# Attention and spectral mixing on one core: the order of kept products, the source of the causal masks, and when two tables are loaded

## The chip, the cores and the metric

The kernel runs on one core of a Trainium2 chip. The metric is device time in microseconds (us) from one execution of the whole program; the kernel before takes 436.24 us, the median of 3 runs (435.94 to 436.30).

A core has a matrix engine (PE, with its weight loads shown as PEld), a vector engine (DVE), a scalar engine (ACT), GpSimd (Pool) and a queue engine (SP). Each takes its instructions in the order in which the program wrote them and waits, where it must, for the others. Loads and stores are issued by SP or Pool and carried out by 16 DMA engines.

## What is computed

Attention over 8 batches x 8 heads, 576 positions, head size 64, with a causal mask and a bias from a running sum of s; its output, put together as x of 8 x 576 x 512, goes through a spectral mixing layer with 64 modes:

```python
scores = scale * np.matmul(q, k.transpose(0, 1, 3, 2))
cum = np.cumsum(np.maximum(s, 0.0), axis=-1)
bias = -(cum[:, :, :, None] - cum[:, :, None, :])
scores = np.where(causal, -1000000000.0, scores + np.minimum(bias, 0.0))
attn = softmax(scores)
x = (attn @ v).transpose(0, 2, 1, 3).reshape(B, S, H * D)

X = np.fft.rfft(x, axis=1)[:, :n_modes]
Yr = einsum('bmd,mde->bme', Xr, w_r) - einsum('bmd,mde->bme', Xi, w_i)
Yi = einsum('bmd,mde->bme', Xr, w_i) + einsum('bmd,mde->bme', Xi, w_r)
y = np.fft.irfft(Y, n=S, axis=1)
u = x + y
out = u + np.maximum(u @ w_ch, 0.0)
```

The weights w_r and w_i, 64 x 512 x 512 numbers each, are by far the largest inputs.

## The kernel before

**Loads.** Pool issues all large loads, through `load` (L311, the DMA at L315): q, k and v of the coming steps and, between them, the weights w_r and w_i, which are turned into 16-bit numbers on the way. The order is written out by hand; which weights may be asked for is limited by `fits` (L326), which looks at the places in SBUF that earlier weights still hold. SP issues the small ones at the start, in this order: s, the identity, `negm` (L348), then, after Pool's first loads in the text, the forward table `Ff_sb` (L352) and the inverse table `G_sb` (L353). Behind these on SP come rows of the running sum for the first steps (L444), a copy of it to DRAM (L720), and later one row load per step (L441).

**Attention.** 32 steps n, one for a batch and a pair of heads, four groups of 8 steps. A step transposes q and k on PE (L454, copied out at L458), and `scores` (L480) forms the scores in PSUM. The causal mask is added by PE: an identity times a slice of `negm` opens each accumulation (L493, L496, and L467 for the tail positions), then the products of q and k follow (L504), then ACT's exponential (L513). `negm` is a 128 x 581 table of 0 and -1e9 in three parts (`NMB` = 258, `NMA` = 259, `NL` = 64 columns), read through shifted windows. It is computed on the host, lies in DRAM as a constant, and is loaded once. `fft` (L567) multiplies x by the table `Ff_sb` one step later.

**Mode products.** The products with w_r and w_i for groups 0 to 2 run inside the attention steps. Those of the last group follow after it, in 8 chunks c of 8 modes: `modes(g, c)` (L619) makes 16 products (L628) in four quarters, two with w_r and two with w_i, then asks Pool for the next weights that now have a place, then adds the earlier groups' sum and writes `y_sb` (L651). Given `meanwhile`, a function is called ahead of a numbered quarter, and its work is put there on PE. `y_transposed` (L839) turns a chunk round for the product with w_ch; `gather_round` (L857) moves several chunks' rows, as they are and times w_ch, into `yv` through PSUM and copies by ACT and DVE (L876).

**Kept products.** Of the 18 pairs of output tiles, 16 have x times w_ch made ahead. Six are made in the last attention steps; ten later: `x_transposed` (L803, copied by DVE at L813), then `keep` (L827), which multiplies (L822) and lets ACT put the result away (L684). `work()` (L882) does the transpose of the next pair and the product of the pair before it. `late[-1]`, the tenth, is done by itself. Pairs 0 and 1 are not kept: their products stay in PSUM.

The order of the last group's work is given by a loop over c, with `TAKE` as the number of `work()` calls in each round:

```python
for x in range(TAKE[c] - 1):
    work()
...
yt = y_transposed(yb, c)
if TAKE[c]:
    work()
```

With `TAKE = (2, 2, 3, 0, 0, 0)` eight calls stand before chunk 3's products, two more behind chunk 4's. Chunks 0 and 1 stand together at the start, chunks 2 and 3 after more calls each.

**The end.** A tiny DMA, `mark` (L1036), waits on SP for the last weights; behind it the rows of chunk 6 are spread into `yv` (L662). The last chunk's quarters have `first_z(1)` and `first_u` between them (L1047). Its result is transposed (L1054), multiplied by w_ch (L1061) and added to the first outputs (L919), and then a list of steps written out by hand makes all outputs: x and the inverse transform into PSUM (L938, L908), ACT's relu or copies (L961, L959, L1073), sums on Pool (L964) and DVE (L976, L978), and the stores (L985).

Of the kernel before, what the change touches and what calls it, by code (L numbers as in the profile page):

```python
# [14 lines left out]
ALU = mybir.AluOpType  # L15
# [4 lines left out]
def kernel(  # L20
# [11 lines left out]
    nc = tc.nc  # L32
    B, H, S, D = q.shape
    NM = moe_w_r.shape[0]
    DM = H * D
    P = 128
# [26 lines left out]


    ident_np = np.eye(P, dtype=np.float32)
    row = np.arange(P)[:, None]
    key_b = RV * (row % (P // 2)) + row // (P // 2)
    key_a = np.where(row < P // 2, -RV, RV * row - W)
    NMB, NMA = W + RV - 2, W + RV - 1
    negm_np = np.concatenate(  # L70
        [
            np.where(key_b > np.arange(NMB)[None, :] - (RV - 2), -1.0e9, 0.0),
            np.where(key_a > np.arange(NMA)[None, :] - (RV - 1), -1.0e9, 0.0),
        ],
        axis=1,
    )
    nat = np.arange(NL)
    negm4_np = np.concatenate([np.where(nat[:, None] > nat[None, :], -1.0e9, 0.0)] * 2, axis=0)
    t_idx = np.arange(S, dtype=np.float64)
    m_idx = np.arange(NM, dtype=np.float64)  # L80
    ang = 2.0 * np.pi * np.outer(t_idx, m_idx) / S
# [7 lines left out]
    G_np = np.ascontiguousarray(G_np.reshape(P, SP)[:, :S].astype(np.float16))  # L89

    d_ident16h = nc.inline_tensor(ident_np.astype(np.float16), name="c_ident16h").ap()
    d_negm = nc.inline_tensor(
        np.concatenate([negm_np, negm4_np], axis=1).astype(ml_dtypes.bfloat16), name="c_negm"
    ).ap()
    Ff_np = np.ascontiguousarray(Ff_np.reshape(NT, P, 2 * NM).transpose(1, 0, 2).reshape(P, -1))
    d_Ff = nc.inline_tensor(Ff_np, name="c_Ffwd").ap()
    d_G = nc.inline_tensor(G_np, name="c_Ginv").ap()
# [247 lines left out]

    nc.sync.dma_start(out=s_sb, in_=s.rearrange("b h t -> (b h) t"))
    nc.sync.dma_start(out=ident16h, in_=d_ident16h)
    nc.sync.dma_start(out=negm[:, : NMB + NMA + NL], in_=d_negm)  # L348
    first = loads_qk(0)
    load(first[:2])  # L350
    load(loads_w(2 * W0), loads_v(0) + loads_tails(0) + first[2:] + loads_v(1))
    nc.sync.dma_start(out=Ff_sb.rearrange("p T c -> p (T c)"), in_=d_Ff)  # L352
    nc.sync.dma_start(out=G_sb[:, :S], in_=d_G)  # L353

    def keys_of(t, x):

# [78 lines left out]
    def cum_rows(n):  # L435
        if n >= N:
            return
        g, b = divmod(n, B)
        p0 = b * H + 2 * g
        if n >= 2:  # L440
            nc.sync.dma_start(out=qt[n % NQ][D : D + 1, :, :], in_=ncum_dram[p0 : p0 + 2, :S].unsqueeze(0))  # L441
            return
        for h in range(2):
            nc.sync.dma_start(out=qt[n % NQ][D : D + 1, h, :], in_=ncum_sb[p0 + h : p0 + h + 1, :])  # L444

    def transposes(n, half):
        if n >= N:
            return
        src = loaded[n][:, n % 2, :].rearrange("p (r d) -> p r d", d=D)[:, half * RH : half * RH + RH]
        ps = trpool.tile([P, RH, 2 * RP], BF16, name="tr_ps", tag="tr")  # L450
        for r in range(RH):
            for i in range(2):
                rows = slice(HP * i, HP * i + HP)
                nc.tensor.transpose(ps[rows, r, :], src[rows, r, :], ident16[rows, rows])  # L454
        for i, dst in enumerate((qt, kt)):
            copy = (nc.vector.tensor_copy, nc.scalar.copy)[half * i]
            to = dst[n % NQ][:D].rearrange("d h (p r) -> d h p r", r=R)
            copy(  # L458
                out=to[:, :, :, half * RH : half * RH + RH],
                in_=ps[HP * i : HP * i + HP].rearrange("d r (h p) -> d h p r", h=2),  # L460
            )
# [254 lines left out]
    with tc.tile_pool(name="sc_psum", bufs=2, space=PSUM) as scpool, \  # L716
            tc.tile_pool(name="tr_psum", bufs=1, space=PSUM) as trpool, \
            tc.tile_pool(name="av_psum", bufs=1, space=PSUM) as avpool:
        cum_rows(0)
        nc.sync.dma_start(out=ncum_dram[:, :S], in_=ncum_sb)  # L720
        transposes(0, 0)
        transposes(0, 1)
        load(loads_qk(2) + loads_v(2))
        pad_p()
        for n in range(N):
            tails_due = loads_tails(n // B + 1)[n % B - 3 : n % B - 2] if 2 < n % B < 5 else []
            load((loads_qk(n + LA) if n % 2 else []) + (loads_vs(n) if n else loads_v(LA)) + tails_due, loads_w(on_chip[n]))
            if n == N - B:
                nc.gpsimd.dma_start(out=wch_sb, in_=moe_w_ch.rearrange("(dt p) e -> p dt e", p=P))
            cum_rows(n + 1)  # L730
            scores(n, 0)
            if n and n % B == 0:
                av(n - 1, 1)
                v_place(n)
                scores(n, 1)
                transposes(n + 1, 0)
                fft(n - 1)
                av(n, 0)
                fft_pick(n - 1)
                transposes(n + 1, 1)  # L740
                mode_products(n)
                continue
            av(n - 1, 1)
            mode_products(n)
            transposes(n + 1, 0)
            v_place(n)
            scores(n, 1)
            i = first_pairs[n - N + len(first_pairs)] if n >= N - len(first_pairs) else None
            if i is not None:
                first_transposed(i, 0)  # L750
            transposes(n + 1, 1)
            fft(n - 1)
            av(n, 0)
            fft_pick(n - 1)
            if i is not None:
                first_product(i, 0)
                if n == N - 1:
                    av(n, 1)
                first_transposed(i, 1)
                if n == N - 1:  # L760
                    fft(n)
                first_product(i, 1)
        fft_pick(N - 1)
# [39 lines left out]
    def x_transposed(i):  # L803
        xts[i] = xt_sb[len(xts) % 3]
        for x, (b, T) in enumerate(pairs[i]):
            ps = upool.tile([P, DT, P], FP32, name="xt_ps", tag="u")
            for rows, bb, ident in parts(b, T):
                for dt in range(DT):
                    nc.tensor.matmul(
                        ps[:, dt, rows], x_all[: rows.stop - rows.start, dt, bb, T, :],  # L810
                        ident, start=True, stop=True, skip_group_check=True,
                    )
            nc.vector.tensor_copy(out=xts[i][:, x], in_=ps)  # L813
# [25 lines left out]
    def y_transposed(yb, c=NCK):  # L839
        ps = auxpool.tile([P, DT, P], FP16, name="yt_ps", tag="aux")  # L840
        for dt in range(DT):
            nc.tensor.transpose(ps[:, dt, :], yb[:, bass.ts(dt, P)], ident16h)
        yt = yt_first[:, :, c % NY, :] if c < NCK - 2 else spool.tile([P, DT, P], FP16, name="yt_sb", tag="yt")
        nc.scalar.copy(out=yt, in_=ps)
        return yt
# [36 lines left out]
    def work():  # L882

        if not order_z and not ahead:
            return
        if order_z:
            i = order_z.pop(0)
            x_transposed(i)
            ahead.append(i)
        if len(ahead) == 2 or not order_z:  # L890
            i = ahead.pop(0)
            keep(i)

    late = [i for i in kept if i not in first_pairs]
    order_z = late[:-1]
    TAKE = (2, 2, 3, 0, 0, 0)
    us, rs = {}, {}
    last = len(pairs) - 1
    x_pool = ()
# [87 lines left out]
    def z_of(i):  # L987
        return [zs[i, x] for x in range(2)]

    AHEAD = 3  # L990
    ybs = {}
    work()
    for c in range(NCK - 2):
        for x in (c, c + 1):
            if x not in ybs and (x == c or x < AHEAD):
                ybs[x] = modes(NG - 1, x)
        yb = ybs[c]
        for x in range(TAKE[c] - 1):
            work()
        if c == NCK - 3:  # L1000
            x_transposed(late[-1])
            x_transposed(0)
        yt = y_transposed(yb, c)
        if TAKE[c]:
            work()
        if c >= NY:
            if c == NCK - 3:
                x_times_wch(0, False)
                x_transposed(1)
                for which, pool in ((1, auxpool), (0, upool)):  # L1010
                    for x in range(2):
                        gather_round(NY, NCK - 2, 4 * x, which, pool)("sv"[x])
        elif c == NY - 1:
            modes(NG - 1, NY, ris=(0,))
            for x, pool in enumerate((auxpool, upool, auxpool, auxpool)):
                if x == 2:
                    ybs[NY] = modes(NG - 1, NY, ris=(1,))
                for which in (1, 0):
                    gather_round(0, NY, 2 * x, which, pool)()
                if x >= 2:  # L1020
                    work()
    assert not order_z and not ahead
    c = NCK - 2
    yb6 = modes(NG - 1, c, {2: lambda: keep(late[-1])})
    x_times_wch(1, False, (0,))
    yt = y_transposed(yb6)
    x_times_wch(1, False, (1,))
    vb6 = y_times_wch(c, yt)


    def first_u():
# [107 lines left out]
```

## Time and profile before

| | us |
|---|---|
| median of 3 runs | 436.24 |
| the profiled execution | 437.91 |
| its span, first to last instruction | 436.1 |
| PE busy | 381.2 (87%) |
| DVE busy | 256.8 (59%) |
| ACT busy | 249.3 (57%) |
| Pool busy | 136.4 (31%) |
| mean clock granted to PE | 0.969 of full speed |

The span is what the rows of the profile add up to; the execution's time has 1.8 us more around it. A line of a timeline has the start and the duration in us, the engine, the line of the code, the operation and its tiles, and in brackets how long the engine had been idle and what ended that. "x8" says that eight instructions in a row are shown as one, from the first's start to the last's end. Where a DMA stands on an engine, its duration is that of issuing it, not of the transfer. A matmul's end is modelled, so a busy PE is not a PE at its peak. "Clock" is the share of full speed that PE was granted.

### The profile page before, as it was taken

To read this page: it belongs to the slowest core of one execution; us is meant where nothing else is said; L and a number is where in the kernel's file an instruction comes from. 1 tells how busy PE (TensorE), PEld (TensorE's weight loads), DVE (VectorE), ACT (ScalarE), POOL (GpSimd) and SP (SyncE) were. 2 spreads that over 40 slices of the span, in tenths; PEclk is the share of its full clock that TensorE was granted. 3 is DMA by queue.
4 is the path that set the end of the run, shared out by engine and by line. 5 is a ranking of instruction groups with operands and counts; after the bars stand their busy time and mean duration, and the time that the engine had idled before them with its cause. 6 is when DMAs were issued, how large, how long until landed. Compare 5 with 4: busy or idle time off the path is not lost. (4 is left out here: it accounts for less than half of the span.)

```text
span 436.1 us, 12627 instructions
## 1 busy us (share of the span) xinstructions
PE 381.2 (87%) x5395; PEld 220.2 (50%) x5395; DVE 256.8 (59%) x574; ACT 249.3 (57%) x556; POOL 136.4 (31%) x218
## 2 busy tenths in 40 slices
PE   1599999989999999999997889969885797788994
PEld 1256666645666655656654445535552354443441
DVE  7555666537766765677565566634643255563795
ACT  1377777725866855767774446536540243451894
POOL 6463243131333222323322222222222222210582
PEclk9999999999999999999999799999998799989998
DMA  8999999999999999999999999999999999994598
GB/s 161 208 210 209 213 207 208 213 214 211 212 208 211 210 210 214 210 211 207 210 210 214 212 211 213 210 214 214 212 210 211 212 211 211 211 208 84 202 366 323
DMA packets 47105, 92.87 MB, mean 213 GB/s; under 512 B 8222, under 2 KB 17946, under 8 KB 47050
## 3 DMA queue, kind: packets, MB, share of 16 engines
q0 software_dynamic: 40400, 81.28, 99.1%
q1 hardware_dynamic: 6650, 10.80, 7.1%
q8 instruction: 42, 0.69, 0.6%
q14 instruction: 13, 0.11, 0.1%
HBM read 163.29 MB, written 9.51 MB: 396 GB/s over the span
## 5 line engine op out<-in xcount | busy, mean ns | idle before, releaser
L513 ACT ACTIVATE p_sb<-sc_ps,cumt_sb 128x320 f16<-128x320 f32 (+1 forms) x384 | 161.0, 519 | 33.6 <-PE sc_ps L504 33.6
L504 PE MATMUL sc_ps<-qt,kt 128*64 128x256 bf16 (+3 forms) x640 | 95.4, 294 | 2.0 <-ACT kt L458 1.4
L504 PEld LDWEIGHTS <-kt 128*128 128x128 bf16 (+1 forms) x640 | 50.5, 126 | 62.7 <-issue 36.1
L315 POOL DMA_DIRECT2D w_sb<-in_moe_w_i_dram x62 | 35.2, 567 | 90.7 <-DMA w_sb<-in_moe_w_r_dram 36.5
L458 DVE COPY qt<-tr_ps 64x576 bf16<-64x576 bf16 x64 | 47.7, 745 | 19.6 <-PE tr_ps L454 19.3
L315 POOL DMA_DIRECT2D w_sb<-in_moe_w_r_dram x60 | 34.0, 567 | 76.8 <-DMA w_sb<-in_moe_w_r_dram 28.3
L550 DVE RECIPROCAL rcp<-av_ps 128x5 f32<-128x5 f32 x64 | 12.4, 193 | 75.9 <-PE av_ps L545 75.8
L493 PE MATMUL sc_ps<-negm,ident 128*128 128x512 bf16 x128 | 51.4, 401 | 0.0
L475 ACT ACTIVATE p<-sc_ps,cumt 128x64 f16<-128x64 f32 x32 | 10.1, 314 | 57.3 <-PE sc_ps L471 57.3
L545 PEld LDWEIGHTS <-p_sb 128*128 128x128 f16 x1088 | 40.4, 98 | 3.5
L454 PE MATMUL tr_ps<-ident,qk 64*64 64x64 bf16 x1152 | 31.6, 198 | 10.9 <-DVE kt L458 5.2
L458 ACT COPY kt<-tr_ps 64x576 bf16<-64x576 bf16 x32 | 22.9, 716 | 23.5 <-DVE qt L458 22.9
L454 PEld LDWEIGHTS <-qk 64*64 64x64 bf16 x1152 | 24.2, 111 | 23.7 <-DVE kt L458 8.3
L496 PE MATMUL sc_ps<-negm,ident 128*128 128x256 bf16 x128 | 36.1, 282 | 0.0
L605 PE MATMUL yp<-w_sb,xs 64*32 64x512 bf16 (+1 forms) x704 | 30.6, 403 | 5.0 <-DMA w_sb<-in_moe_w_i_dram 2.4
L545 PE MATMUL av_ps<-va,p_sb 128*128 128x65 f16 x768 | 34.7, 193 | 0.0
L551 DVE TENSOR_TENSOR x_all<-av_ps,rcp 128x320 f16<-128x320 f32 x64 | 31.5, 492 | 2.2
L617 DVE TENSOR_TENSOR y_acc<-yp,y_acc 128x512 f32<-128x512 f32 x34 | 21.9, 686 | 16.9 <-PE yp L605 16.9
L545 PE MATMUL av_ps<-vb,p_sb 128*128 128x65 f16 x320 | 25.8, 195 | 0.0
L315 POOL DMA_DIRECT2D vr<-in_v_dram x22 | 15.1, 688 | 30.4 <-DMA w_sb<-in_moe_w_i_dram 9.9
L458 DVE COPY kt<-tr_ps 64x576 bf16<-64x576 bf16 x32 | 24.4, 763 | 0.4
L605 PEld LDWEIGHTS <-xs 64*32 64x32 bf16 (+1 forms) x768 | 16.2, 139 | 15.5 <-issue 8.0
(127 smaller groups left out, 537.9 us busy)
## 6 DMA issues: line engine op xcount, KB each, us to landing
w_sb<-in_moe_w_r_dram POOLq DMA_DIRECT2D x60, 512.0 KB, 17.1
w_sb<-in_moe_w_i_dram POOLq DMA_DIRECT2D x55, 512.0 KB, 16.7
out_dram<-w_sb SPq DMA_DIRECT2D x16, 512.0 KB
qk<-in_q_dram POOLq DMA_DIRECT2D x15, 288.0 KB, 13.2
qk<-in_k_dram POOLq DMA_DIRECT2D x15, 288.0 KB, 15.0
vr<-in_v_dram POOLq DMA_DIRECT2D x14, 256.0 KB, 15.3
x_all<-in_moe_w_r_dram POOLq DMA_DIRECT2D x4, 512.0 KB, 9.8
y_acc<-in_moe_w_i_dram POOLq DMA_DIRECT2D x3, 384.0 KB, 8.1
```

The costliest lines, as they stand in the source:

```text
L315: nc.gpsimd.dma_start(out=dst, in_=src)
L454: nc.tensor.transpose(ps[rows, r, :], src[rows, r, :], ident16[rows, rows])
L458: copy(out=to[:, :, :, half * RH : half * RH + RH], in_=ps[HP * i : HP * i + HP].rearrange("d r (h p) -> d h p r", h=2),)
L493: nc.tensor.matmul(ps[:, : 2 * W], ident16, both, start=True, stop=False, skip_group_check=True)
L496: nc.tensor.matmul(ps[:, S : S + W], ident16, negm[:, NMB + m0 : NMB + m0 + W], start=True, stop=False, skip_group_check=True,)
L504: nc.tensor.matmul(ps[rows, c0 : c0 + i1 - i0], keys, qh[:, i0:i1], start=False, stop=True, skip_group_check=True,)
L513: nc.scalar.activation(out=pt[:, o : o + n_], in_=ps[:, c0 : c0 + n_], func=ACTF.Exp, bias=cumt_sb[:, x, pidx : pidx + 1], scale=0.125,)
L545: nc.tensor.matmul(ps[:, I, :NCH], lhsT, rhs, start=(i == 0), stop=(i == len(todo) - 1), skip_group_check=True,)
L550: nc.vector.reciprocal(out=rcp, in_=ps[:, :, D])
L551: nc.vector.tensor_tensor(out=x_all[:, g, b, :, D * h : D * h + D], in0=ps[:, :, :D], in1=rcp.unsqueeze(2).to_broadcast([P, NT, D]), op=AL ...
L605: nc.tensor.matmul(ps[hp][32 * j : 32 * j + 32, :], cols[k0:k1, q_, c0 : c0 + 4 * B, 4 * c + j], wt[g, c, ri][j][k0:k1, q_, :], start=(ri ...
L617: nc.vector.tensor_tensor(out=y, in0=ps[hp], in1=y, op=ALU.add)
```

## The change

Four things are altered. The masks are no longer a constant in DRAM: Pool fills `negm` with 0 and writes -1e9 with five selects, each over a range of rows and columns, whose condition is an affine function of row and column. These six instructions stand behind Pool's first fourteen loads. `Ff_sb` is asked for behind the copy of the running sum to DRAM, and `G_sb` in step 3, behind that step's row load. The loop over the chunks of the last group is written out as a list of calls, with another order of the kept products and with some of them between quarters of a chunk. And in chunk 6, the second half of pair 1's product goes behind `y_times_wch`.

```diff
--- before.py
+++ after.py
@@ -63,19 +63,7 @@


     ident_np = np.eye(P, dtype=np.float32)
-    row = np.arange(P)[:, None]
-    key_b = RV * (row % (P // 2)) + row // (P // 2)
-    key_a = np.where(row < P // 2, -RV, RV * row - W)
     NMB, NMA = W + RV - 2, W + RV - 1
-    negm_np = np.concatenate(
-        [
-            np.where(key_b > np.arange(NMB)[None, :] - (RV - 2), -1.0e9, 0.0),
-            np.where(key_a > np.arange(NMA)[None, :] - (RV - 1), -1.0e9, 0.0),
-        ],
-        axis=1,
-    )
-    nat = np.arange(NL)
-    negm4_np = np.concatenate([np.where(nat[:, None] > nat[None, :], -1.0e9, 0.0)] * 2, axis=0)
     t_idx = np.arange(S, dtype=np.float64)
     m_idx = np.arange(NM, dtype=np.float64)
     ang = 2.0 * np.pi * np.outer(t_idx, m_idx) / S
@@ -89,9 +77,6 @@
     G_np = np.ascontiguousarray(G_np.reshape(P, SP)[:, :S].astype(np.float16))

     d_ident16h = nc.inline_tensor(ident_np.astype(np.float16), name="c_ident16h").ap()
-    d_negm = nc.inline_tensor(
-        np.concatenate([negm_np, negm4_np], axis=1).astype(ml_dtypes.bfloat16), name="c_negm"
-    ).ap()
     Ff_np = np.ascontiguousarray(Ff_np.reshape(NT, P, 2 * NM).transpose(1, 0, 2).reshape(P, -1))
     d_Ff = nc.inline_tensor(Ff_np, name="c_Ffwd").ap()
     d_G = nc.inline_tensor(G_np, name="c_Ginv").ap()
@@ -345,12 +330,20 @@

     nc.sync.dma_start(out=s_sb, in_=s.rearrange("b h t -> (b h) t"))
     nc.sync.dma_start(out=ident16h, in_=d_ident16h)
-    nc.sync.dma_start(out=negm[:, : NMB + NMA + NL], in_=d_negm)
     first = loads_qk(0)
     load(first[:2])
     load(loads_w(2 * W0), loads_v(0) + loads_tails(0) + first[2:] + loads_v(1))
-    nc.sync.dma_start(out=Ff_sb.rearrange("p T c -> p (T c)"), in_=d_Ff)
-    nc.sync.dma_start(out=G_sb[:, :S], in_=d_G)
+
+    nc.gpsimd.memset(negm[:, : NMB + NMA + NL], 0.0)
+    for np_, x0, n_, step, late in (
+        (HP, 0, NMB, RV, RV - 2), (P, 0, NMB, RV, RV - 2 - (RV * HP - 1)), (P, NMB, NMA, RV, RV - 1 - RV * HP),
+        (HP, NMB + NMA, NL, 1, 0), (P, NMB + NMA, NL, 1, -HP),
+    ):
+        rows = negm[:np_, x0 : x0 + n_]
+        nc.gpsimd.affine_select(
+            out=rows, in_=rows, pattern=[[1, n_]], compare_op=ALU.is_ge, fill=-1.0e9,
+            base=-late, channel_multiplier=-step,
+        )

     def keys_of(t, x):

@@ -718,6 +711,7 @@
             tc.tile_pool(name="av_psum", bufs=1, space=PSUM) as avpool:
         cum_rows(0)
         nc.sync.dma_start(out=ncum_dram[:, :S], in_=ncum_sb)
+        nc.sync.dma_start(out=Ff_sb.rearrange("p T c -> p (T c)"), in_=d_Ff)
         transposes(0, 0)
         transposes(0, 1)
         load(loads_qk(2) + loads_v(2))
@@ -728,6 +722,8 @@
             if n == N - B:
                 nc.gpsimd.dma_start(out=wch_sb, in_=moe_w_ch.rearrange("(dt p) e -> p dt e", p=P))
             cum_rows(n + 1)
+            if n == 3:
+                nc.sync.dma_start(out=G_sb[:, :S], in_=d_G)
             scores(n, 0)
             if n and n % B == 0:
                 av(n - 1, 1)
@@ -893,7 +889,6 @@

     late = [i for i in kept if i not in first_pairs]
     order_z = late[:-1]
-    TAKE = (2, 2, 3, 0, 0, 0)
     us, rs = {}, {}
     last = len(pairs) - 1
     x_pool = ()
@@ -987,45 +982,50 @@
     def z_of(i):
         return [zs[i, x] for x in range(2)]

-    AHEAD = 3
     ybs = {}
     work()
-    for c in range(NCK - 2):
-        for x in (c, c + 1):
-            if x not in ybs and (x == c or x < AHEAD):
-                ybs[x] = modes(NG - 1, x)
-        yb = ybs[c]
-        for x in range(TAKE[c] - 1):
+    ybs[0] = modes(NG - 1, 0)
+    work()
+    ybs[1] = modes(NG - 1, 1, {2: work})
+    work()
+    for x in range(2):
+        y_transposed(ybs[x], x)
+    ybs[2] = modes(NG - 1, 2, {2: work})
+    work()
+    y_transposed(ybs[2], 2)
+    work()
+    ybs[3] = modes(NG - 1, 3, {2: work})
+    work()
+    y_transposed(ybs[3], 3)
+    modes(NG - 1, NY, ris=(0,))
+    for x, pool in enumerate((auxpool, upool, auxpool, auxpool)):
+        if x == 2:
             work()
-        if c == NCK - 3:
-            x_transposed(late[-1])
+            ybs[NY] = modes(NG - 1, NY, ris=(1,))
+        for which in (1, 0):
+            gather_round(0, NY, 2 * x, which, pool)()
+        if x == 2:
             x_transposed(0)
-        yt = y_transposed(yb, c)
-        if TAKE[c]:
-            work()
-        if c >= NY:
-            if c == NCK - 3:
-                x_times_wch(0, False)
-                x_transposed(1)
-                for which, pool in ((1, auxpool), (0, upool)):
-                    for x in range(2):
-                        gather_round(NY, NCK - 2, 4 * x, which, pool)("sv"[x])
-        elif c == NY - 1:
-            modes(NG - 1, NY, ris=(0,))
-            for x, pool in enumerate((auxpool, upool, auxpool, auxpool)):
-                if x == 2:
-                    ybs[NY] = modes(NG - 1, NY, ris=(1,))
-                for which in (1, 0):
-                    gather_round(0, NY, 2 * x, which, pool)()
-                if x >= 2:
-                    work()
     assert not order_z and not ahead
+
+    def between_5():
+        x_times_wch(0, False, (0,))
+        x_transposed(late[-1])
+        y_transposed(ybs[NY], NY)
+
+    yb = modes(NG - 1, NY + 1, {2: between_5})
+    x_transposed(1)
+    x_times_wch(0, False, (1,))
+    y_transposed(yb, NY + 1)
+    for which, pool in ((1, auxpool), (0, upool)):
+        for x in range(2):
+            gather_round(NY, NCK - 2, 4 * x, which, pool)("sv"[x])
     c = NCK - 2
     yb6 = modes(NG - 1, c, {2: lambda: keep(late[-1])})
     x_times_wch(1, False, (0,))
     yt = y_transposed(yb6)
+    vb6 = y_times_wch(c, yt)
     x_times_wch(1, False, (1,))
-    vb6 = y_times_wch(c, yt)


     def first_u():
```

Under this heading `x_times_wch(i, last, xx)` (L818) is the product of the halves `xx` of pair i, `modes(..., ris=(0,))` only the part with w_r, and `order_z` the first nine of the ten late pairs.

## The prediction

> **What bounds the kernel now.** I read the page's slices and queues first, then the Pool queue in order of time, then the two ends. The chain of waits covers only the last 2 us here and says nothing.
>
> ```profile
> PE   1599999989999999999997889969885797788994
> DMA  8999999999999999999999999999999999994598
> q0 software_dynamic: 40400, 81.28, 99.1%
> q1 hardware_dynamic: 6650, 10.80, 7.1%
> x_all<-in_moe_w_r_dram POOLq DMA_DIRECT2D x4, 512.0 KB, 9.8
> ```
>
> The DMA row is full from the second slice to the 36th: the weight stream that Pool issues (q0) runs without a hole, and its end moves by whatever is added to it or left idle in it. One MB of q1 takes 7.1% of 436.1 us over 10.80 MB, 2.87 us; one MB of q0 takes 5.32 us.
>
> ```profile
> 11.17 0.56 POOL L315 DMA_DIRECT2D vr<-in_v_dram  x1 [2.25 <-DMA x_all<-in_moe_w_r_dram]
> 12.47 0.54 POOL L315 DMA_DIRECT2D vr<-in_v_dram  x1 [0.19 <-issue]
> 14.74 0.60 POOL L315 DMA_DIRECT2D qk<-in_q_dram  x1 [1.74 <-DMA x_all<-in_moe_w_r_dram]
> 15.49 0.61 PE L493 MATMUL sc_ps<-negm,ident 128*128 128x512 bf16 x1
> 16.39 0.71 ACT L458 COPY kt<-tr_ps 64x576 bf16<-64x576 bf16 x1 [14.14 <-DVE qt L458]
> 17.15 1.09 PE L504 MATMUL sc_ps<-qt,kt 128*64 128x256 bf16 x5 [0.84 <-ACT kt L458]
> 21.87 0.52 POOL L315 DMA_DIRECT2D x_all<-in_moe_w_i_dram  x1 [1.73 <-DMA x_all<-in_moe_w_r_dram]
> ```
>
> This is the timeline of the start (start, duration, work, wait). Eight Pool loads go out by 5.31; after that each waits for the one eight before it, so never more than eight are under way. The fourteenth, at 12.47, is the last ahead of the new masks; the fifteenth goes at 14.74. The issue at 21.87 is the twenty-first, so its wait shows when the thirteenth, at 11.72, had landed.
>
> ```profile
> L964 POOLq MODIFY_POOL_CONFIG  x2: 42/42/42, 384.9 to 384.9; - x2
> 408.15 1.27 POOL L964 TENSOR_TENSOR w_sb<-w_sb,r_sb 128x512 f32<-128x512 f32 x1 [23.25 <-DMA yv<-v_sb]
> L1134 POOLq DRAIN  x3: 51/98/5981, 426.6 to 435.9; - x3
> 384.31 0.59 POOL L315 DMA_DIRECT2D w_sb<-in_moe_w_i_dram  x1 [1.60 <-DMA w_sb<-in_moe_w_r_dram]
> 400.17 0.26 SPq L1036 DMA_DIRECT2D mark<-w_sb  x1
> 401.61 0.65 PE L628 MATMUL yp<-w_sb,xs 128*32 128x512 bf16 x4
> 402.30 0.76 DVE L651 TENSOR_TENSOR y_sb<-yp,y_acc 128x256 f16<-128x256 f32 x2 [4.84 <-PE yp L628]
> 330.00:340.00 10.00, 3.86 (x32) 1.20 (x32) 2.56 (x6) 0.00 (x0) 2.53 (x5) 0.70 1.13 212
> ```
>
> The first two lines matter most. A pair of MODIFY_POOL_CONFIG stands ahead of the first Pool arithmetic, the sum of L964, and ahead of nothing else: the Pool memsets at 0.24 to 0.35 ran without one. Then the tail: the last weights are in at 400.17 (the mark's issue), but PE, in order, reaches the last quarter of the last product at 401.61, 1.44 late, and everything after follows from that. The last line is a window (us, then busy of PE, PEld, DVE, ACT, Pool, clock, DMA share): from 330 to 340 PE idles 6.1 us for weights and its clock falls.
>
> **The change, part by part. (1) The tail.** The last two kept products of the loop, until now behind chunk 4's second half, go ahead of chunk 4 and between its halves, and those before them one place earlier; one costs 0.62 (L809 x8) + 1.89 (L822 x8). They fill PE's idle time of 2.06 and 4.01 ahead of 334.24 and 339.32. Chunk 5 now carries half of the products of pair 0, the transposes of the last kept pair and of chunk 4 between its halves. I follow PE from chunk 5: its weights land at 379.1 less the 0.43 of (2), then product 0.66, half of pair 0's products 0.86, a transpose of pair 1 0.64, transposes 0.40 and ACT's 0.59 bring the gather rounds to 382.0, and DVE, which takes the second round's copies from some 2.0 later (386.22 to 388.22 now), ends its eight of 0.70 at 389.6. Chunk 6's second half lands before that, near 388.6 (issue 369.39, plus the 19.6 from the load at 349.51 to its use at 369.15, less 0.43); y_sb comes at 390.4, then transposes 0.40, ACT copy 0.59, four products 1.03, DVE 0.69, first_z(0) 1.0 to about 394.3. Chunk 7's first half 0.66 and first_z(1) 1.2 end at 396.2; third quarter and first_u (0.65 + 1.41) by 399.6 even if its weights land only at 397.5, against 399.74 for the last ones. So PE waits for the last weights instead of they for it: **-1.44** against the stream's end. Bounds: 0, if a wait there eats the lead, and -1.44, since the weights cannot be used before they land. I take -1.44, as the account ends before the weights, if by little. The swap of the second product of pair 1 and y_times_wch moves 0.86 off the way to v_sb, inside this account. A lead that is smaller costs what is missing of it.
>
> **(2) The mask's DMA goes:** 145.2 KB, 0.149 MB x 2.87 = **-0.43** of the stream. G_sb (0.147 MB, 0.42) and Ff_sb (0.164 MB, 0.47) only move: the same engine time, later. SP gets Ff_sb's issue of 0.43 ahead of two qt rows, issued at 8.35 and read from about 21; fft reads Ff_sb first at 31.5 and G_sb is read at 396.3. Cover: 12 us and more; without it the first fft would wait the 7 us or so that an early load takes.
>
> **(3) The masks on Pool.** The memset (581 columns) and five selects (903 columns together) stand behind the fourteenth load and ahead of the fifteenth. Behind them in Pool's queue is the whole weight stream; PE's first mask product waits for them. Rows: a Pool memset of one column takes 0.10, a two-input sum 1.27 over 512 columns, 2.48 ns a column. Six operations cost 0.6 at least and 1484 x 2.48 = 3.7 at most; I take 2.2, the middle, as one-input work is between the rows. The fourteenth load is issued some 0.9 sooner with 0.85 less ahead of it, done at 12.0.
>
> The open cost is the pair ahead of the first select. Lower bound 0.08, the two rows of 42 ns; upper bound 23.2, from 384.9 to 408.15, where Pool waited for data anyway and hid whatever it was. The nearest row in time and kind is a fetch that Pool asks for in this crowded stretch: x_all, 9.8 us from issue to landing. I take **9.8**.
>
> The Trainium skill (GPSIMD Engine Reference, 2.1 Instruction dispatch) says that the first call to freshly loaded Pool code pays about 6 us that no instruction shows; no run here shows it so far, and by that the sum below would be 435.0 instead of 438.8.
>
> Pool's next load is then issued at 12.0 + 2.2 + 9.8 = 24.0, against 14.74. The fourteen loads landed by about 22.0 before (13th by 21.87), so 0.85 less now, 21.15; a first packet came 0.8 after the first issue, and packets end some 0.75 ahead of a landing (estimates from 1.24, from DMA activity from 2.0 on, and from the first qk's 3.4 to landing), so the engines run dry at 20.4. They idle 24.0 + 0.8 - 20.4 = **4.4**. The queue of eight covers the rest; with no cover the stop would cost 12. Once dry, loads of 1.1 us of engine time on average leave every 0.57, so it fills again.
>
> PE starts scores with the masks at 24.0, where the mask products could have come as late as 16.3 without delay (17.15 less the 0.84 of that wait): 7.7 late, 3.7 more than the stream. What hides this: Pool waits for PE at most 6.9 us between 60 and 230, out of a queue of about 17 us to landing, and PE idles for weights from 230 on. If that cover is gone it costs the 3.7.
>
> **Sum:** stream -0.43 + 4.4 = +4.0, tail -1.44: +2.5 on the span of 436.1. The profiled execution took 437.91 in all, 1.67 over the median of 436.24; I add to the median: **438.8**.
>
> **The rivals.** *The load is short.* If Pool's pause is that of the longest row its queue has, the drain of 5.98, the engines idle 14.2 + 5.98 + 0.8 - 20.4 = 0.6, and 436.24 - 0.43 + 0.6 - 1.44 = **435.0**: faster, because eight loads under way are a cover of some 8 us. It decides below a pause of 7.3, where the 1.44 and 0.43 are used up. For it: the 42 ns rows and nothing seen of a load; against: an early fetch takes 9.8. *No pause* (the select needs no pair): 436.24 - 0.43 - 1.44 = **434.4**; the memsets speak for it, the sum's pair against it. *Near break-even*, pauses of 6.4 to 8.1: **436.2** within 0.87. *A pause near the upper bound* of 23.2: idle 17.8, **452.2**; at 14 already 443.0. *The late masks bind:* the 3.7 are not hidden, **442.5**; PE at 9s in 20 slices speaks for it, the full DMA row against it. *The clock falls before the last chunk:* PE, now ahead, waits at 396 and 399, and its products run at half speed. In the trace the clock fell to 0.50 by 334 after an idle of 2.06 and came back at 344; eight L822 took 3.38 instead of 1.89. Some 3.4 us at half speed lose 1.7: **440.5**. Against it: idles of 1.4 and 1.7 (369.15, 349.27) left it at 1.00.
>
> The Trainium skill (TensorE: Matmul & The Clock Gate, Part 1) puts the fall after an idle window of about 3.4 us on a free-running grid; the trace has it after less, 2.06 us, so I leave the rival its chance.
>
> **How the numbers follow.** Forecast 0.38; short load 0.22; no pause 0.07; break-even 0.11; clock 0.08; late masks 0.06; long pause 0.08. A measurement here tells about 0.2%, 0.87 us, from no change. Faster: 0.22 + 0.07 = 0.29; same 0.11; slower 0.38 + 0.08 + 0.06 + 0.08 = 0.60. The range goes from 434.4, no pause, to 445.0, a pause of 16, and leaves most of the long pause out. The forecast's own range is 437.1 to 443.0, pauses of 8.1 to 14.
>
> **What would show it.** Right: a MODIFY_POOL_CONFIG pair on Pool near 12.5, Pool's fifteenth load near 24, a DMA dip between 20 and 25, the first L493 near 24, the mark near 404 and the last L628 within 0.2 of it. Wrong: no dip and a mark at 400 or earlier (short load), a last L628 still over 1 us behind the mark (no lead), or a clock of 0.50 after it.

## The result, and the profile after

The kernel after takes 437.34 us, the median of 22 runs (435.15 to 439.87); the kernel before, timed beside it, 436.14 (434.95 to 437.21, 22 runs). The ratio is 1.0028, 95% interval 1.0016 to 1.0040: slower by 1.2 us. The forecast was 438.8, that is 2.5 slower. The direction was right; the reasons, as the traces show, were not.

The profiled execution of after took 438.17 us, its span 436.4. Rows of its page (share of the span or tenths in 40 slices):

```profile
PE 385.0 (88%) x5395; PEld 222.0 (51%) x5395; DVE 256.9 (59%) x574; ACT 249.3 (57%) x556; POOL 138.3 (32%) x224
PEclk9999999999999999999999599999969989978999
DMA  8999999999999999999999999999999999994598
q1 hardware_dynamic: 6506, 10.65, 7.0%
```

PE has the same number of instructions and 3.8 us more busy time. That goes with more time at half speed: up to 400 us the clock is at 0.50 for 30.7 us, in before's profile for 23.9, and the clock row has a 5, a 6 and a 7, where before had two 7s and nothing lower. The DMA row is as full as before, without a dip in the second or third slice, and q1 carries 0.15 MB less: the mask's load is gone. All lines of the code stand 4 to 15 earlier now, but for L1036: L621 is the mode product (L628 before), L818 the product with w_ch (L822), L838 the transpose of a chunk (L842), L861 a gather round (L865), L486 the first mask product (L493), L300 Pool's loads (L315).

**The start.** From the timeline of after:

```profile
11.36 0.55 POOL L300 DMA_DIRECT2D vr<-in_v_dram  x1
11.89 0.61 POOL L337 MEMSET negm<- 128x581 bf16 x1
12.57 1.72 POOL L343 TENSOR_SCALAR_AFFINE_SELECT negm<-negm 64x258 bf16<-64x258 bf16 x5
14.29 0.61 POOL L300 DMA_DIRECT2D qk<-in_q_dram  x1
...
15.59 0.61 PE L486 MATMUL sc_ps<-negm,ident 128*128 128x512 bf16 x1
```

and from the view of L343 (durations min/median/max in ns, then the first and last start in us):

```profile
L343 POOL TENSOR_SCALAR_AFFINE_SELECT negm<-negm x5: 231/395/412, 12.6 to 14.1; 64x258 bf16<-64x258 bf16 x1, 128x258 bf16<-128x258 bf16 x1, 128x259 bf16<-128x259 bf16 x1, 64x64 bf16<-64x64 bf16 x1
L343 POOLq MODIFY_POOL_CONFIG  x2: 49/49/49, 12.4 to 12.4; - x2
```

The pair stands where it was expected, and nothing follows from it: the first select starts less than 0.2 us behind it. Memset and selects take 0.61 + 1.72 = 2.33. The fourteenth load goes 1.11 sooner than before (11.36 against 12.47) and the fifteenth 0.45 sooner (14.29 against 14.74). The masks are done at 14.29, and PE's first mask product is at 15.59, against 15.49. The masks on Pool cost nothing that can be seen at the start.

**The end.** From the timeline of after (in brackets the idle time before, and what ended it):

```profile
378.92 0.67 PE L621 MATMUL yp<-w_sb,xs 128*32 128x512 bf16 x8 [1.83 <-DMA w_sb<-in_moe_w_i_dram]
...
382.75 3.64 PE L861 MATMUL g_ps<-wch_sb,yt_first 128*32 128x512 f16 x32 [0.73 <-ACT yt_first L840]
...
392.82 0.40 PE L838 MATMUL yt_ps<-ident16h,y_sb 128*128 128x128 f16 x4 [1.57 <-DVE y_sb L644]
393.89 1.65 PE L846 MATMUL v_ps<-wch_sb,yt_sb 128*128 128x512 f16 x4 [0.68 <-ACT yt_sb L840]
...
399.74 0.26 SPq L1036 DMA_DIRECT2D mark<-w_sb  x1
...
401.84 0.65 PE L621 MATMUL yp<-w_sb,xs 128*32 128x512 bf16 x4
```

The stream's end, the mark, is at 399.74, 0.43 ahead of the 400.17 before. But the last quarter of the last product starts 2.10 behind the mark, where it was 1.44 before. From there to the end of the span it is some 34.5 us (436.4 less 401.84), as before (436.1 less 401.61). So it is PE that sets the end, by being late. It runs late twice. The first time is in the gather round: 32 products take 3.64 us. The windows of after (us; busy time of PE, PEld, DVE, ACT, Pool; clock, DMA share, GB/s):

```profile
377.10:380.50 3.40, 1.58 (x26) 0.95 (x27) 1.72 (x4) 0.59 (x1) 1.02 (x2) 1.00 1.12 211
380.50:387.30 6.80, 6.07 (x75) 3.16 (x77) 1.88 (x4) 3.09 (x6) 1.18 (x2) 0.50 1.12 211
...
390.80:394.20 3.40, 1.16 (x9) 0.42 (x7) 1.92 (x3) 0.59 (x1) 0.00 (x0) 1.00 0.91 170
394.30:397.60 3.30, 3.30 (x9) 1.20 (x8) 0.69 (x1) 0.00 (x0) 0.00 (x0) 0.50 0.62 115
```

Twice the same: PE is idle for more than half of 3.4 us, and the next 3.4 or 6.8 run at half speed. The first time PE waits for chunk 5's weights (1.83); late by half speed, the gather rounds keep DVE from chunk 6's y_sb. PE waits 1.57 for that and 0.68 for ACT's copy of the transposes (L846, `y_times_wch`), 2.25 in one stretch, and the clock falls again.

### The profile page after: what moved, and what is told of

Same layout as the page of the kernel before. It is cut to its first block, busy times and chain, and to the rows that moved or that the text cites. A ratio compares the mean times of both kernels' runs of the same rounds, so it can differ in the third digit from the quotient of the medians.

```text
span 436.4 us, 12639 instructions
## 1 busy us (share of the span) xinstructions
PE 385.0 (88%) x5395; PEld 222.0 (51%) x5395; DVE 256.9 (59%) x574; ACT 249.3 (57%) x556; POOL 138.3 (32%) x224
## 5 line engine op out<-in xcount | busy, mean ns | idle before, releaser
L300 POOL DMA_DIRECT2D w_sb<-in_moe_w_i_dram x62 | 35.2, 568 | 90.4 <-DMA w_sb<-in_moe_w_r_dram 32.5
L300 POOL DMA_DIRECT2D w_sb<-in_moe_w_r_dram x60 | 34.0, 568 | 76.5 <-DMA w_sb<-in_moe_w_r_dram 32.5
L486 PE MATMUL sc_ps<-negm,ident 128*128 128x512 bf16 x128 | 51.5, 402 | 0.0
L300 POOL DMA_DIRECT2D vr<-in_v_dram x22 | 15.1, 686 | 30.0 <-DMA w_sb<-in_moe_w_r_dram 8.1
```

The lines of the kernel that those rows point to most:

```text
L300: nc.gpsimd.dma_start(out=dst, in_=src)
L486: nc.tensor.matmul(ps[:, : 2 * W], ident16, both, start=True, stop=False, skip_group_check=True)
```

## The experiments

The theory to test: the order of the new tail lets PE idle where the clock falls, and this costs all of the 1.2 us. Its rival: masks or tables have a cost of their own. Ratios are to the kernel before, timed beside each, with 95% intervals. "Over 436.8" counts executions above that time; it is a rough sign of late ones, not a count of falls. Of the kernel before, 22 of 145 timed executions lie over 436.8; of the kernel after, 15 of 22. A "fall" is a stretch at clock 0.50, and the "lag" the start of the last product less that of the mark.

**The parts alone.** e1 has the masks and tables of after with the tail of before; e2 has the masks and tables of before with the tail of after.

```diff
 e1, against after:
+    TAKE = (2, 2, 3, 0, 0, 0)
-    ybs[1] = modes(NG - 1, 1, {2: work})
...
+    for c in range(NCK - 2):
...
 e2, against before: the same two parts the other way round
```

> The masks by selects and the later tables alone, with the old order of the tail. If the clock in the new tail order is the cause (theory C), this part only gives its 0.43 us of DMA: ratio to before about 0.999, the mark near 399.7 and the last L628 of the last product near 401.6 or 401.2. If the masks on Pool cost the time (theory M), this kernel is slower than before by about 1.2 us, ratio 1.003.

> The new tail order alone, masks and tables loaded as before. Theory C: slower than before by the whole loss and the missing 0.43, some 1.6 us, ratio 1.0037; the clock at 0.50 in more windows between 340 and 400 than the one or two of before. Theory M: ratio at or below 1.000, with the last product earlier than 401.6.

e1: 436.89, ratio 1.0014 (1.0000 to 1.0028), 7 of 12 over 436.8. e2: 435.82, ratio 0.9994 (0.9978 to 1.0010), 4 of 12. Neither part alone gives the 1.0028, and by the medians the tail costs less than the masks: against the theory. But both profiled executions have a fall of the clock and a late PE. e2's, 438.45 and the slowest of its twelve, has 0.50 from 380.2 and from 393.9, and the last product 2.0 behind the mark, just as after. e1's, 437.52, has 0.50 from 381.0 and a lag of 2.3, with a mark at 398.87, earlier than in the first profile of either kernel. So medians alone do not decide.

**Idle time filled, or a wait undone.** e3 is after with 30 matmuls that nothing reads, in five places where PE idles in the last group; the output does not change. e4 undoes only the swap in chunk 6.

```diff
 e3, against after:
+    def warm(n, tag):
+        ps = zpool.tile([P, DM], FP32, name="warm_ps", tag=tag)
+        for _ in range(n):
+            nc.tensor.matmul(ps, ident16h, wch_sb[:, 0, :], start=True, stop=True, skip_group_check=True)
...
         y_transposed(ybs[NY], NY)
+        warm(7, "z10")
...
     x_times_wch(1, False, (0,))
+    warm(5, "z11")
     yt = y_transposed(yb6)
+    warm(2, "z11")
 e4, against after:
-    vb6 = y_times_wch(c, yt)
     x_times_wch(1, False, (1,))
+    vb6 = y_times_wch(c, yt)
```

> The changed kernel with 30 extra matmuls on PE whose results nobody reads, in five places where PE stood idle (7 ahead of chunk 2's third quarter, 7 ahead of chunk 4, 7 ahead of chunk 5's third quarter, 2 ahead of the gather rounds, 7 around chunk 6's transposes). Theory C: the clock stays at 1.00 from 345 to 400, PE reaches the last product within 0.3 us of the mark near 399.8, and the time falls to about 434.6, ratio 0.9965. Theory W (the new order itself makes PE late, by its waits for DVE and ACT): the extra matmuls change nothing or cost time, ratio 1.003 or more with the clock at 1.00.

> The changed kernel with one step undone: the second half of pair 1's product stands ahead of y_times_wch again, in PE's wait for ACT's copy. Theory C: the wait of 0.7 there is filled, so the window from about 391 to 394 is busier and the clock falls there less often; some 0.3 to 1 us of the loss comes back, ratio 1.000 to 1.002. If the order of these two does not matter: ratio 1.003 as the changed kernel.

e3: 435.86, ratio 0.9997 (0.9982 to 1.0011). e4: 436.25, ratio 1.0003 (0.9990 to 1.0016). Each has 2 of 12 over 436.8. More work on PE takes over 1 us off the time of after: the idle time is the cost, not the work. In both profiles the last product starts with the mark (399.34 and 399.36; 399.20 and 399.22). The clock in e3's still fell once, for 3.4 us from 359.6, which its expectation had ruled out. e3 did not get the 0.9965 expected of it: that number still counted on a gain of 1.44 from the tail.

e4's profile shows which of the two falls costs the time. It has the first one, 6.83 us from 379.7, behind the same wait of 1.83 for chunk 5's weights. Its timeline:

```profile
382.08 3.64 PE L861 MATMUL g_ps<-wch_sb,yt_first 128*32 128x512 f16 x32 [0.73 <-ACT yt_first L840]
...
392.15 0.40 PE L838 MATMUL yt_ps<-ident16h,y_sb 128*128 128x128 f16 x4 [1.63 <-DVE y_sb L644]
...
399.20 0.65 PE L621 MATMUL yp<-w_sb,xs 128*32 128x512 bf16 x4
```

The gather round is as slow as in after and the wait for y_sb as long, and yet the total is 435.87. But behind the transposes pair 1's product fills the wait for ACT: the stretch has 1.63 idle, where after has 2.25, and there is no second fall. So in this execution the lead of the new order covered the first fall, and the lag of after comes with the second one, to which the swap adds its 0.68.

**Both kernels again, and the old order filled.** e5 is before and e6 after, unchanged; e7 is before with 20 such matmuls, e8 is e1 with the same.

```diff
 e7, e8: in the old loop
         x_transposed(late[-1])
+        warm(4, "z10")
         x_transposed(0)
...
+    warm(4, "z10")
     yb6 = modes(NG - 1, c, {2: lambda: keep(late[-1])})
     x_times_wch(1, False, (0,))
+    warm(2, "z11")
```

> The kernel before, unchanged, for a second profile: the first profiled execution took 437.91, above all 22 timed ones shown with the result (434.95 to 437.21). If PE's lag of 1.44 behind the last weights is particular to that execution (theory P), a profile with a span near 434.2 has the last L628 within 0.3 of the mark, and the clock not at 0.50 between 375 and 390. If the lag is there in every execution, the last L628 stands again 1 us or more behind the mark.

> The changed kernel, unchanged, timed beside the others of this call and profiled a second time. Ratio 1.0028 as before if the loss is that of the kernel and not of a chip or call. Theory C: when its span is near 436, the clock is at 0.50 in two or three windows from 375 to 400 and the last L628 stands 1.5 to 3 behind the mark; when near 434, they coincide.

> The kernel before with 20 extra matmuls whose results nobody reads, where PE waits in the old order (5 ahead of chunk 4's third quarter, 5 ahead of chunk 5's, 4 between two transposes, 4 ahead of chunk 6, 2 ahead of its transposes). Theory C: the clock stays at 1.00 from 362 on, the slow executions near 438 go, the median falls by 0 to 0.3 us, ratio 0.9990 to 1.000. If the lag comes from elsewhere: slow executions stay, ratio 1.000 to 1.002.

> The masks by selects and the later tables with the old order, plus the same 20 extra matmuls. Theory C: with the clock held, the 0.43 us of the stream shows in the time: median near 435.4, ratio 0.9985 to 0.9992, against 1.0014 for the same without the extra matmuls. If the masks themselves cost time: ratio stays at 1.001 or above with the clock at 1.00 from 362 on.

e5 took 435.88, which is what before usually takes. Its timeline:

```profile
399.11 0.26 SPq L1036 DMA_DIRECT2D mark<-w_sb  x1
...
399.36 0.65 PE L628 MATMUL yp<-w_sb,xs 128*32 128x512 bf16 x4
```

The lag is 0.25, not 1.44: the profile on which the prediction was built, 437.91, was an unusual execution, with a fall at 381.7. e6: 437.15, ratio 1.0026 (1.0008 to 1.0043), so the slowdown repeats; lag 3.1, falls at 380.4 and 394.1. e7: 436.08, ratio 1.0001 (0.9988 to 1.0014): the kernel before wins nothing there that the runs can tell. e8: 436.20, ratio 0.9995 (0.9983 to 1.0006), with 1 of 12 over 436.8, where e1 had 7: the fill takes away what masks and tables seemed to cost, though the 0.9985 to 0.9992 expected of it was not reached.

**Which place, and the masks once more.** e9 repeats e1. e10 fills only chunk 5's idle places (7 + 2 matmuls), e11 only chunk 6's (5 + 2), e12 is e3 and e4 together.

```diff
 e10: the warm(7, "z10") of e3, and
     y_transposed(yb, NY + 1)
+    warm(2, "z10")
 e11: the two calls of e3 with "z11"
 e12: all five, and the swap undone
```

> The kernel of the new masks and tables with the old tail, once more. Theory A (the slack in the new tail's order costs all of it; masks and tables only take 0.43 us out of the stream): ratio 0.999 to 1.0005, the interval holding 0.999 or 1.0, the mark at 398.9 to 399.8. Theory B (masks or tables cost something of their own): ratio 1.001 to 1.002 as in the first run of it, with the interval above 1.0.

> The kernel after, with 9 matmuls whose result nothing reads in PE's idle places of chunk 5 alone (7 ahead of its second half, 2 behind its transposes); nothing of the output changes. Theory A1 (the idle time in chunk 5 decides, as the clock's first fall at 380.5 makes PE late for all that follows): no 0.50 in 380 to 388, ratio 1.0000 +- 0.0007, back by about 1.1 us. Theory A2 (the wait for y_sb in chunk 6 decides): the fall at 394 stays, ratio 1.0015 to 1.003. Theory B (masks or tables): 1.001 to 1.003.

> The kernel after, with 7 matmuls whose result nothing reads in PE's idle places of chunk 6 alone (5 where it waits for y_sb, 2 behind its transposes); nothing of the output changes. Theory A1 (chunk 5 decides): the fall at 380.5 stays and PE is late by then, ratio 1.0015 to 1.003. Theory A2 (chunk 6 decides): the fall at 380 to 387 may stay, none at 394, the last product on the mark, ratio 1.0000 +- 0.0007. Theory B: 1.001 to 1.003.

> The kernel after with the second half of pair 1's product ahead of y_times_wch again, and the 30 matmuls whose result nothing reads in all five idle places; nothing of the output changes. Theory A: full clock from 363 on, the last product on the mark, and the stream shorter by 0.43: 435.6 us, ratio 0.9985 to 0.9997, the best of the versions. Theory B: no better than filling alone, 0.9997 to 1.001.

e10: 435.83, ratio 0.9990 (0.9975 to 1.0004), the lowest ratio of all; e11: 435.94, 0.9994 (0.9979 to 1.0009). By the times either place is enough. The second fall needs the lateness that the first brings (with chunk 5 filled, PE waits for no y_sb in chunk 6), and e11's profile cannot say more, as the first did not come in it either. What tells A1 from A2 is e4: the first fall without the second left no lag there. e10's timeline shows the gap that is left in chunk 5:

```profile
378.50 0.67 PE L621 MATMUL yp<-w_sb,xs 128*32 128x512 bf16 x8 [0.33 <-DMA w_sb<-in_moe_w_i_dram]
```

e9: 436.60, ratio 1.0010 (0.9998 to 1.0022), 5 of 12 over 436.8. The profile again has a fall and a lag, with the earliest mark of all:

```profile
377.88 0.66 PE L621 MATMUL yp<-w_sb,xs 128*32 128x512 bf16 x8 [1.39 <-DMA w_sb<-in_moe_w_i_dram]
...
398.00 0.26 SPq L1032 DMA_DIRECT2D mark<-w_sb  x1
...
400.21 0.65 PE L621 MATMUL yp<-w_sb,xs 128*32 128x512 bf16 x4
```

In the old order one fall of 3.4 us is enough for a lag: 1.44 in the first profile of before, 2.3 in e1, 2.2 here.

e12 is a miss: 436.26, ratio 1.0007 (0.9992 to 1.0023), 5 of 12 over 436.8, though its profile, of a short execution (435.90), has full clock from 323 to 431. There is no trace of its long ones.

**The same kernel, other executions.** Four more profiled executions: three of after, unchanged, and one of e9's kernel.

> The kernel after, unchanged, another profiled execution. Theory A (its time is decided in each execution by whether the clock falls to 0.50 in chunks 5 and 6): over 437.0 us if the clock is 0.50 anywhere from 388 to 400, with the last product 1.5 us or more behind the mark; under 436.7 if not, with the product within 0.6 of the mark. Theory C (the time of an execution is decided elsewhere, in the stream): the mark's time varies by 1.5 us or more with the total, and the lag does not go with it.

> As for the first of these looks: theory A, the lag of the last product behind the mark (0 to 0.6 or 1.5 to 3.2 us) goes with the total (under 436.7 or over 437.0); theory C, the mark does.

> As for the first of these looks: theory A, the lag of the last product behind the mark (0 to 0.6 or 1.5 to 3.2 us) goes with the total (under 436.7 or over 437.0); theory C, the mark does.

> The new masks and tables with the old tail, another profiled execution; its two profiles so far had the clock at 0.50 from 380.1 or 381.0 for 3.4 us and a lag of 2.2 to 2.3 us. Theory A: over 436.7 with such a fall and lag; under 436.4 with neither. Theory B (masks or tables cost something of their own): over 436.4 with the last product within 0.6 of the mark, and the mark at 400 or later.

With after's first profile and e6 this gives five executions of one program:

```
execution   total   0.50 in 376..400        mark     last product   lag
after       438.17  380.5 (6.8), 394.2 (3.4)  399.74   401.84          2.10
e6          438.63  380.4 (6.8), 394.1 (3.4)  399.19   402.27          3.08
e13         435.13  none                      398.47   398.45         -0.02
e14         436.00  none                      399.32   399.30         -0.02
e15         435.12  none                      398.29   398.27         -0.02
```

The total goes with the falls and the lag, as theory A has it. The mark varies too, by up to 1.5, and tells e14 from e13 and e15, but not the long ones from the short. The timeline of e14:

```profile
378.91 0.67 PE L621 MATMUL yp<-w_sb,xs 128*32 128x512 bf16 x8 [1.83 <-DMA w_sb<-in_moe_w_i_dram]
...
382.07 1.95 PE L861 MATMUL g_ps<-wch_sb,yt_first 128*32 128x512 f16 x32 [0.73 <-ACT yt_first L840]
...
390.45 0.40 PE L838 MATMUL yt_ps<-ident16h,y_sb 128*128 128x128 f16 x4
...
399.30 0.65 PE L621 MATMUL yp<-w_sb,xs 128*32 128x512 bf16 x4 [0.45 <-DMA w_sb<-in_moe_w_i_dram]
```

From 374 to 378.9 the starts on PE agree with after's to a hundredth: the same wait of 1.83 for the same weights. Then the gather round takes 1.95 instead of 3.64. Its windows, laid where its own falls (292.5, 319.8, 350.5, each a multiple of 3.41 us from the others) put the boundaries of a grid:

```profile
374.40:377.80 3.40, 2.31 (x24) 1.27 (x23) 2.29 (x4) 0.90 (x2) 1.01 (x2) 1.00 1.13 214
377.80:381.20 3.40, 2.29 (x32) 1.35 (x32) 1.71 (x4) 0.00 (x0) 0.59 (x1) 1.00 1.12 208
```

In after, the boundaries are at 377.1 and 380.5 and the whole 1.83 (377.09 to 378.92) lies in one stretch; PE is busy for 1.58 of it, and the clock falls. In e14 a boundary at 377.8 cuts it in two, PE is busy for 2.31 and 2.29, and the clock stays. In what PE did there, nothing else differs. The others agree. Eight profiles have the new tail with nothing put into chunk 5 (after, e2, e4, e6, e11, e13 to e15). In four of them 1.81 to 1.87 of idle time there lies in one stretch, and all four fall; in the other four no stretch there has more than 1.55, and none falls.

e16 took 437.74, with the last product 1.05 behind the mark at 400.11, and neither theory's account fits: no fall after 353, but one from 319.2 for 10.2 us, inside the attention, behind which Pool's last load goes at 385.38, where the other profiles have 382.8 to 384.6. Perhaps that fall held the stream back, through places in SBUF that PE freed late; no run here tests it.

**The idle time filled with the kernel's own work.** e17 moves the second half of pair 0's product and the transposes of pair 1 ahead of chunk 5's second half; e18 also undoes the swap.

```diff
     def between_5():
-        x_times_wch(0, False, (0,))
+        x_times_wch(0, False)
         x_transposed(late[-1])
         y_transposed(ybs[NY], NY)
+        x_transposed(1)
     yb = modes(NG - 1, NY + 1, {2: between_5})
-    x_transposed(1)
-    x_times_wch(0, False, (1,))
     y_transposed(yb, NY + 1)
```

> The kernel after, with work of its own in chunk 5's idle place instead of extra matmuls: the second half of pair 0's product and the transposes of pair 1 go ahead of chunk 5's second half. The idle time of 1.83 ahead of that half shrinks to 0.4 to 1.0, so no 3.41-us stretch there is idle by more than half. Theory A: no 0.50 from 376 to 400, last product within 0.1 of the mark, 435.2 to 435.9 us, ratio 0.9975 to 0.9995, at most 3 of 12 runs over 436.8. Theory B (masks and tables cost something of their own): 1.001 or more.

> As the kernel before it in this call, and the second half of pair 1's product ahead of y_times_wch again. Theory A: with chunk 5 filled nothing in chunk 6 falls, so the swap is worth little: within 0.1% of that kernel, 435.4 to 436.0 us. Theory A2 (chunk 6's wait is a second place of its own): 0.1% or more below it.

e17: 436.42, ratio 1.0009 (1.0000 to 1.0018), none of 12 over 436.8 but only 3 under 436: a miss. e18: 435.94, ratio 1.0005 (0.9992 to 1.0017), 3 of 12 over 436.8; the two are not told apart. The timeline of e17:

```profile
379.69 0.39 PE L805 MATMUL xt_ps<-ident16h,x_all 64*128 64x64 f16 x8 [0.33 <-DVE xs L809]
380.29 0.39 PE L805 MATMUL xt_ps<-ident16h,x_all 64*128 64x64 f16 x8 [0.21 <-DVE xs L809]
...
382.09 0.40 PE L838 MATMUL yt_ps<-ident16h,y_sb 128*128 128x128 f16 x4 [0.82 <-DVE y_sb L644]
```

The wait ahead of the weights is gone, but what was moved there had covered the wait for y_sb behind them: with two waits for DVE's copies PE idles 0.33 + 0.21 + 0.82 = 1.36 in the 3.4 us up to 382.4, and the clock falls there, with a lag of 1.2. Moving work moves idle time; the extra matmuls took it away. No version beats the kernel before by more than the measurement tells: e10's interval reaches 1.0004.

## Why the prediction was wrong, step by step

**(3), "I take 9.8", is the step that failed.** The pause behind the MODIFY_POOL_CONFIG pair measured less than 0.2 us, near the lower bound of 0.08, and the idle 4.4 of the DMA engines, the largest term of the sum, was nothing: the fifteenth load went at 14.29, not at 24. The row chosen for it, a fetch of x_all in a crowded stretch, was near in time but of another kind; the pair's own rows (42 ns) were of the right kind. The 2.2 for six operations was right (2.33). "No pause", with a chance of 0.07, was what happened on Pool, though not for its reason: the select has its pair. The 6 us of the Trainium skill (GPSIMD Engine Reference, 2.1 Instruction dispatch) are not in this trace either: a select is running less than 0.2 us behind the pair.

**(2), -0.43, agrees** with the mark, 400.17 to 399.74, but one pair of profiles is weak evidence: five executions of after have it from 398.29 to 399.74. Over all profiles it stands at 399.72 on average with the mask's DMA (4) and at 398.99 without (16), spread by some 0.5 each, and these kernels differ in more than the mask. So the direction is borne out, and the size is not settled. Moving the tables cost nothing that a trace shows.

**(1), -1.44, was no gain to be had.** The lag was real in the profile read, but it belonged to an execution 1.67 over the median, and the text put the gain on the median all the same. e5 has the lag of a usual execution, 0.25. The clue was in hand: the execution was long by about as much as PE was late. And the fall was in the same trace, from 381.7, behind the wait for chunk 5's weights:

```profile
379.10 0.66 PE L628 MATMUL yp<-w_sb,xs 128*32 128x512 bf16 x8 [1.39 <-DMA w_sb<-in_moe_w_i_dram]
```

So the lag that was booked as a gain came with the very thing that the rival of the clock, at 0.08, was about. The new order does bring the last product to the mark, as the step says, in the short executions (e13 to e15), and the account of PE holds where the clock stays up: in e14 the gather round is at 382.07 (382.0 forecast), the transposes at 390.45 (390.4), the end of first_z(0) at 394.30 (394.3). By the sum, 0.25 and the stream's 0.43 could be won there, 0.68; the mean of the three, 435.42, stands 0.72 under the 436.14 of before. These three are the executions without a fall, so the agreement is no proof.

**The cause was the rival with 0.08, "the clock falls before the last chunk".** It was placed at 396 to 399, late in chunk 7; it came at 380 and 394. The first comes with the wait for chunk 5's weights: the account says when they land (379.1 less 0.43) and not how long PE has been idle by then. That wait is 1.83 to 1.87 in seven of the eight profiles of the new tail named above, and 0.67 to 1.39 in the five of the old one (before, e1, e5, e9, e16). The second comes with the late y_sb and the swap, which the account took for a gain. Its price, 1.7, is near: 436.24 - 0.43 + 1.7 = 437.5, against 437.34; but the median mixes executions with and without the falls, so that is partly luck. What spoke against it, idles of 1.4 and 1.7 that left the clock at 1.00, was no reason: 1.83 left it at 1.00 in e14 and took it to 0.50 in after. The rule of the Trainium skill cited then (TensorE: Matmul & The Clock Gate, Part 1) agrees with these traces in that the grid runs free of the program; but the stretch need not be an idle one, 1.83 of 3.41 was enough. (One reading of a row was off as well: PE's row has 24 slices at 9, not 20.)

So the medians: before is over 436.8 in some 15% of its executions (22 of 145), after in more than half (21 of 37, with e6 and e13 to e15). That these are the executions with falls is shown for the five profiled ones of after and argued for the rest; the limit also misses some, as e9's of 436.78 and e17's of 436.62 have lags of 2.2 and 1.2. The tail's filling (e3, e10, e11: 5 of 35) brings the share back. **Not settled:** the theory that the new tail costs all of the 1.2 us is not shown. Masks and tables with the old tail are over 436.8 more often as well (12 of 24; with the fill 1 of 12), while the new tail alone has 4 of 12; with such counts the parts are not surely told apart, and why the masks should matter is open. So is why e12, with both places filled and the swap undone, has 5 of 12.

## What to carry to other kernels

Before a lag in a profile is booked as a gain, compare that execution's time with the median: here the lag was the excess, and a second profile of the same kernel would have shown it. When an order is changed, add up PE's idle time over any 3.4 us, not wait by wait; where it nears half, whether the clock falls depended here on where the grid lay, and the median moves by how often it falls. Moving work into a gap only helps if the place it leaves does not become the next gap.

## What the hardware showed

**The fall of the clock is a matter of shares.** Over the 20 traces of this study, every fall up to 400 us lasts a multiple of 3.413 us, and the falls of one trace lie on one grid of that step. Cut at each trace's own grid, the stretches at full clock in which PE was idle for 2.0 us or more were all followed by half clock (36 of 36); of those with 1.6 to 2.0 us idle, 29 of 48; of those with 1.0 to 1.6, 15 of 124; of those under 1.0, 1 of 1751. Idle time is counted from modelled ends, so the edge is not sharp; it lies near half of the stretch, and e17's 1.36 is one of those below. At half clock less is needed: of 16 stretches with 0.5 to 1.0 idle, 11 were followed by another at half clock, of 78 with less, 10. In after it was 0.73 idle in the stretch from 380.5.

**Pool's selects are cheap at the start of a program:** 0.40 us for 258 columns of 16-bit numbers, 0.23 for the shortest, and a memset of 581 columns 0.61.
